# Turning 64 of 96 octets in the second half of batch 0, more zero products in the front, and two tiles' values in a row

## The chip, the cores and the metric

The kernel runs on one core of a Trainium2 chip. The metric is the time of one execution in microseconds; the number that counts is the median over several runs. The span is the time from the first to the last instruction on the core, which the profile sees; the time of a run also has what lies around it.

## The reference

There are four batches, eight heads, 768 positions and 64 numbers per head. Attention goes by chunks of 32 positions: each chunk sees 8 memory keys, its own 32 positions, 16 before and 8 after. A feed-forward part follows.

```python
for c in range(24):
    k_full = concat(mem_k, k[16 before .. 8 after the chunk]); v_full likewise
    a = softmax(q[chunk] @ k_full.T / 8)
    x[chunk] = a @ v_full                     # 8 heads side by side: 512 wide
xn = (x - mean) / sqrt(var + 1e-6) * g_ln
out = x + relu(xn @ w_ch1) @ w_ch2            # 512 -> 2048 -> 512
```

## The kernel before, in words

The 4 x 768 positions make 24 tiles of 128. Three tiles are a unit, so there are eight units, two to a batch. All matmul inputs are 16-bit; sums stand in PSUM in 32 bits.

**Attention of a tile.** `scores` (L278) forms, for two groups of 64 positions, keys times queries into an `att` buffer of PSUM; ScalarE takes the exponentials into `AT` (L294). `values` (L302) multiplies them with `V` into another `att` buffer; a column of ones in `V` gives the sums. `norm` (L314) divides on VectorE (L317, L318), takes the mean (L324) and writes `xn` (L327). `root` (L331) gets the variance: the squares on ScalarE (L333), the inverse root on GpSimd (L336, L340). `turn_x` (L342) turns `xn` into `xT`, in units 0 and 1 with four transposing matmuls (L350) and a copy on ScalarE (L355), later with a DMA. The two `att` buffers are handed out in turn by `slot`, so a product into one waits for whatever still reads it.

**Turning k and q.** `scores` needs k and q with the head's numbers along the partitions. For batches 0 and 1 they are loaded with an octet of positions to a partition (96 octets). `turn_kq` (L183) turns them with a 64-column weight per head and position-in-octet, against the identity, two heads at once in the two column halves of the array: 16 transposing matmuls for a pair of heads. `keep_k` (L195, VectorE) and `keep_q` (L208, ScalarE) then copy out of PSUM into `KT` and `QT`. The first half of batch 0 (octets 0 to 63 for k, 0 to 47 for q) is done in the front. `kq_block` (L215) does the rest of batch 0 in two blocks (128 matmuls) after step 15 of unit 0: it turns all 96 octets, and copies groups 6 to 11 (k from 7).

**The feed-forward of a unit.** Sixteen steps of `up` (L368): four matmuls each and a ReLU, on VectorE and ScalarE in turn (L383, L381). Then twelve steps of `down` (L387), four matmuls each. In unit 0 the order of `down` is by parts: steps 16 to 18 do part 0 of the three tiles and read the first quarter of `w2c`, steps 19 to 21 the second, 22 to 24 the third, 25 to 27 the fourth. The last part adds `xs` on VectorE (L399) and sends the tile out.

**The order of work** is written out by hand. A dictionary `plan` holds, per step of a unit, what is issued after that step's `up` or `down`. `attend` places scores, values, norm and turn_x of the following unit's tiles from four step numbers per tile, and root three steps after turn_x. Each engine runs its instructions in the order of issue.

**The front** (L455 to L562) does the first half of batch 0 and the attention of tiles 0 to 2. `stay_busy` (L360) issues products of zeros (`busy`, 128 x 512) whose result nothing reads. The front's norms, turns and first `up` steps follow one another from tile to tile.

**Loads** are issued on GpSimd's queue in a fixed order (L462 to L505): k and q of the first half, V groups 0 to 5, the four pieces of `w1c`, the second half of k and q, `w2c` 0 and 1, V groups 6 to 9, `w2c` 2, V groups 10 and 11, `w2c` 3. At most eight are under way: the next issue waits until an earlier one has landed.

Of the kernel before, what the change touches and what calls it, by code (L numbers as in the profile page):

```python
# [15 lines left out]
def kernel(  # L16
# [12 lines left out]
    nc = tc.nc  # L29
# [13 lines left out]
    identity = sb.tile([128, 128], FP16, name="identity")  # L43
# [17 lines left out]
    k16 = [t[0:96, 0:4096].rearrange("p (h r d) -> p h r d", h=H, r=8) for t in kraw]  # L61
    q16 = [t[0:96, 0:4096].rearrange("p (h r d) -> p h r d", h=H, r=8) for t in qraw]
# [17 lines left out]
    att = [ps.tile([128, 2, 512], FP32, name=f"att{i}") for i in range(2)]  # L80
# [11 lines left out]
    def free(ap, off, pattern, parts=None):  # L92

        p = list(ap.ap[0]) if parts is None else [ap.ap[0][0], parts]
        return bass.AP(tensor=ap.tensor, offset=ap.offset + off, ap=[p] + [list(x) for x in pattern])

    def as16(t):
        return t.bitcast(FP16)
# [76 lines left out]
    def mem_cols(b):  # L175
        src = memKT[:, 4 * b : 4 * b + 4, :]
        nc.vector.tensor_copy(
            out=free(KT[b % 2], 96, [[KW, 4], [4 * KW, NG], [1, 8]]),
            in_=bass.AP(tensor=src.tensor, offset=src.offset,
                        ap=[list(src.ap[0]), [8, 4], [0, NG], [1, 8]]),  # L180
        )

    def turn_kq(pv, src, j, n):  # L183

        for r in range(8):
            for par in range(2):
                nc.tensor.matmul(  # L187
                    out=pv[64 * par : 64 * par + 64, n * r : n * r + n],
                    lhsT=src[0:n, 2 * j + par, r, :],
                    rhs=identity[0:n, 0:n],  # L190
                    is_transpose=True, start=True, stop=True,
                    tile_position=(0, 64 * par),
                )

    def keep_k(pv, b, j, n, g0, g1, copy=nc.vector.tensor_copy):  # L195

        for ga, gb in ((0, 1), (1, NG - 1), (NG - 1, NG)):
            ga, gb = max(ga, g0), min(gb, g1)
            if ga < gb:
                lo = 0 if ga == 0 else 8 * ga - 2  # L200
                m = 10 if gb == NG else 8 * ga + 9 - lo
                copy(
                    out=free(KT[b % 2], (4 * ga + j) * KW + 16 + 8 * (lo - 8 * ga),
                             [[4 * KW, gb - ga], [8, m], [1, 8]]),
                    in_=free(pv, lo, [[8, gb - ga], [1, m], [n, 8]]),
                )

    def keep_q(copy, pv, b, j, n, g0, g1):  # L208

        copy(  # L210
            out=free(QT[b % 2], (4 * g0 + j) * 64, [[256, g1 - g0], [8, 8], [1, 8]]),
            in_=free(pv, 8 * g0, [[8, g1 - g0], [1, 8], [n, 8]]),
        )

    def kq_block(b, j, g0, g1, kind):  # L215

        pk, pq = slot("att"), None
        if kind == "att":
            pq = slot("att")
            pq = [pq[:, i, :] for i in range(2)]  # L220
        else:
            pq = [slot("mm")[:, :] for i in range(2)]
        for i in range(2):
            turn_kq(as16(pk[:, i, :]), k16[b % 2], j + i, 96)
        for i in range(2):
            turn_kq(as16(pq[i]), q16[b % 2], j + i, 96)

        def keep(i):
            keep_k(as16(pk[:, i, :]), b, j + i, 96, g0 + 1 if g0 else 0, g1)
            keep_q(nc.scalar.copy, as16(pq[i]), b, j + i, 96, g0, g1)  # L230

        keep(0)
        kept_later.append(lambda: keep(1))
# [126 lines left out]
    def stay_busy(n, p=None):  # L360

        p = slot("mm") if p is None else p
        for _ in range(n):
            nc.tensor.matmul(out=p, lhsT=busy[:, 0:128], rhs=busy, start=True, stop=True)  # L364
# [107 lines left out]
    clear_v(0, nc.vector, lambda: clear_k(0), 33)  # L472
    mem_keys()
    mem_cols(0)
    for g in range(3):
        load_v_group(0, g)

# [21 lines left out]
    for g in range(10, NG):  # L499
# [3 lines left out]
        out=memv16[:, 1:B, :, 0:64],  # L503
# [15 lines left out]
        keep_k(first_k[j], 0, j, CUT[0], 0, 7)  # L519
        keep_q(act, first_q[j], 0, j, CUT[1], 0, 6)  # L520
    keep_mem(0, 0, 6, vec)
    stay_busy(3, spare)
    for j in range(2, 4):
        turn_kq(first_k[j], k16[0], j, CUT[0])
    stay_busy(4, spare)
# [8 lines left out]
    vec(out=g_row, in_=banks[2])  # L534
    scores(0, 0)
    scores(0, 1)
    stay_busy(2)
    values(0, 0)
    norm(0, 0)
    stay_busy(3)  # L540
# [24 lines left out]
    for u, tiles in enumerate(units):  # L565
        n = len(tiles)
        following = units[u + 1] if u + 1 < len(units) else []
        plan = {}

        def at(step, fn, *args):  # L570
            plan.setdefault(step, []).append((fn, args))

        def attend(steps, kind="dma"):

            for i, (s0, s1, s2, s3) in enumerate(steps):
                t = following[i]
                at(s0, scores, t // 6, t % 6)
                at(s1, values, t // 6, t % 6)
                at(s2, norm, t % 6, t % 9)
                at(s3, turn_x, u + 1, i, t % 6, kind)  # L580
                at(min(s3 + 3, 27), root, t % 6, t % 9)

        def cross(steps, b, t0, t1, t2):

            for half in range(2):
                at(steps[half], cross_k, b, half, t0, t1)
                at(steps[2 + half], cross_q, b, half, t2 - 3, t2)

        if u == 0:
            at(9, clear_k, 1)  # L590
            at(11, keep_mem, 0, 6, NG, vec)
            at(13, nc.vector.memset, V[0].bitcast(FP32)[:, :, :, 33 : HD // 2], TWO_ONES)
            at(14, nc.vector.memset, memv16[:, :, :, 64:HD], 1.0)
            at(23, clear_v, 1, nc.gpsimd)
            for j in (0, 2):
                at(15, kq_block, 0, j, 6, NG, "mm")
                at(15, keep_rest)
            for t in range(3):
                at(19 + t, root, t, t)
            for h in (0, 4):  # L600
                for which in range(2):
                    at(15, load_kq, 1, which, 0, 96, h, h + 4)
            for g in range(6):
                at(23, load_v_group, 1, g)
            attend(((17, 19, 19, 22), (17, 21, 21, 24), (20, 23, 23, 26)), "att")
            at(26, mem_cols, 1)
            at(26, v_mem, 1)
        elif u == 1:
            for j in (0, 2):
                at(5 + 3 * j, kq_block, 1, j, 0, NG, "att")  # L610
                at(7 + 3 * j, keep_rest)
            for g in range(6, NG):
                at(0, load_v_group, 1, g)
            for t in range(6):
                for which in range(2):
                    at(14, load_tokens, 2, which, t)
            attend(((16, 19, 19, 22), (16, 19, 20, 23), (21, 23, 23, 26)), "att")
        elif following:
            if u in (2, 4):
                attend(((2, 7, 7, 7), (2, 7, 8, 8), (9, 13, 13, 13)))  # L620
            else:
                attend(((9, 14, 14, 14), (9, 14, 15, 15), (16, 20, 20, 20)))
            if u == 2:
                cross((0, 0, 1, 1), 2, 0, 4, 3)
                at(8, mem_cols, 2)
                at(8, k_around, 2, 0, 4)
                for h in range(H):
                    at(8, load_v_head, 2, h)
                cross((14, 14, 15, 15), 2, 4, 6, 6)
            elif u == 3:  # L630
                at(1, v_mem, 2)
                at(1, v_around, 2)
                at(4, k_around, 2, 4, 6)
                for t in range(6):
                    for which in range(2):
                        at(24, load_tokens, 3, which, t)
            elif u == 4:
                for h in range(H):
                    at(0, load_v_head, 3, h)
                cross((14, 14, 15, 15), 3, 0, 4, 3)  # L640
                at(17, mem_cols, 3)
                at(17, v_mem, 3)
                at(17, v_around, 3)
                at(22, k_around, 3, 0, 4)
                cross((20, 21, 24, 25), 3, 4, 6, 6)
            elif u == 5:
                at(2, k_around, 3, 4, 6)
        for step in range(16 + 4 * n):
            if step < 16:
                if u or step > 7:  # L650
                    up(u, n, step)
            else:
                i, part = divmod(step - 16, 4)
                if u == 0:
                    i, part = (step - 16) % 3, (step - 16) // 3
                if following or i < n - 1:
                    down(tiles[i], i, part)
                elif part == 0:
                    down_last(tiles[i], i)
            for fn, args in plan.get(step, ()):  # L660
                fn(*args)
# [30 lines left out]
```

The softmax here doesn't subtract the row's maximum and nothing guards it: scores larger than these inputs give would overflow.

## Time and profile before

| what | us |
|---|---|
| median of 5 runs | 216.72 |
| lowest, highest | 214.76, 219.79 |
| the profiled execution | 216.99 |
| its span, first to last instruction | 215.3 |
| TensorE matmuls busy | 208.9 |
| VectorE, ScalarE, GpSimd busy | 113.5, 91.2, 91.9 |

The mean granted TensorE clock over the span is 0.992 of full speed. Software DMAs (GpSimd's queue) moved 14.38 MB, the others 12.54 MB.

Reading it: lines of the timeline give the start in us, the time from the first start to the last end, engine, line of the kernel, operation, output and inputs with their shapes, and how many instructions the row holds; brackets give the idle time of that engine before it, and what ended it. Matmuls are pipelined, so that the cost of a row is best read from the start of one row to the start of the next. "PE" is TensorE's products, "PEld" its weight loads, "DVE" VectorE, "ACT" ScalarE, "POOL" GpSimd. An answer on DMAs gives their number, size and the time from issue to landing.

### The profile page before, as it was taken

The page shows a single profiled execution, that of the slowest core. Times are in us where ns is not written, and L with a number is a line of the kernel's source. Part 1 is how long each engine was busy: PE and PEld are TensorE (multiplying, and loading weights), DVE is VectorE, ACT ScalarE, POOL GpSimd, SP SyncE. Part 2 cuts the span into 40 slices and gives each one's busy share as a digit, 9 for nine tenths or more (in the row PEclk, how much of TensorE's full clock was granted, in tenths as well). Part 3 has the DMA queues.
Part 4 walks back from the last instruction along what each step waited for, and adds up shares of the span by engine and source line. Part 5 has one row for each costly group of instructions (what it writes and reads, how often), then busy time and mean ns, then how long its engine had stood idle before and what let it go on. Part 6 is the DMA issues. An engine that isn't in the chain of part 4 may idle for free.

```text
span 215.3 us, 5336 instructions
## 1 busy us (share of the span) xinstructions
PE 208.9 (97%) x2173; PEld 124.1 (58%) x2173; DVE 113.5 (53%) x268; ACT 91.2 (42%) x187; POOL 91.9 (43%) x169
## 2 busy tenths in 40 slices
PE   7889999999999999999999999999999999999993
PEld 2545876457755566546654566446644665456553
DVE  4657484585757548524385349324474437534222
ACT  4254535954573676301653067203661265303200
POOL 7992236489999228810004999520042000400000
PEclk9988999999999999999999999999999999999999
DMA  5999999999999959995405999997496201230012
GB/s 77 164 123 201 204 215 182 195 206 229 151 137 171 144 144 128 119 186 156 65 15 87 136 175 155 138 161 113 115 137 184 77 3 24 80 119 0 0 52 97
DMA packets 87611, 27.26 MB, mean 127 GB/s; under 512 B 78289, under 2 KB 84081, under 8 KB 87538
## 3 DMA queue, kind: packets, MB, share of 16 engines
q0 software_dynamic: 62128, 14.38, 74.7%
q1 hardware_dynamic: 25458, 12.54, 27.2%
q8 instruction: 17, 0.28, 0.6%
q14 instruction: 8, 0.07, 0.1%
HBM read 28.84 MB, written 6.29 MB: 163 GB/s over the span
## 4 chain that ended last, share of the span: by engine, by line
PE 91%; DVE 2%; DMA 2%; POOL 1%; issue 1%; ACT 1%; POOLq 0%; DVEq 0%; ACTq 0%
PE mm L375 38%; PE mm L392 38%; PE att L307 4%; PE att L287 3%; DMA kraw<-in_k_dram 2%; PE att L187 2%; PE mm L364 2%; PE mm L410 2%; PE mm L187 1%; DVE xn L327 1%; DVE xs L318 1%; PE att L350 1%; ACT AT L294 1%; PE mm L533 0%; PE att L364 0%
## 5 line engine op out<-in xcount | busy, mean ns | idle before, releaser
L375 PE MATMUL mm<-xT,w1c 128*128 128x384 f16 (+2 forms) x528 | 87.9, 322 | 0.1
L392 PE MATMUL mm<-w2c,rT 128*128 128x512 f16 x368 | 84.2, 379 | 0.0
L375 PEld LDWEIGHTS <-w1c 128*128 128x128 f16 x528 | 57.9, 114 | 24.8 <-issue 0.6
L381 ACT ACTIVATE rT<-mm 128x384 f16<-128x384 f32 (+2 forms) x66 | 31.7, 484 | 75.3 <-PE mm L375 53.9
L392 PEld LDWEIGHTS <-rT 128*128 128x128 f16 x368 | 34.5, 98 | 38.4
L383 DVE TENSOR_SCALAR rT<-mm 128x384 f16<-128x384 f32 (+2 forms) x66 | 35.6, 542 | 33.7 <-PE mm L375 33.4
L399 DVE SCALAR_TENSOR_TENSOR osb<-mm,rstd,xs 128x512 f32<-128x512 f32 x23 | 17.3, 751 | 42.2 <-PE mm L392 30.9
L294 ACT ACTIVATE AT<-att,band 104x512 f16<-104x512 f32 x48 | 29.5, 688 | 11.9 <-PE att L287 10.2
L336 POOL TENSOR_SCALAR veps<-squares 128x1 f32<-128x1 f32 x24 | 5.1, 213 | 50.0 <-ACT junk L333 48.7
L116 POOL DMA_DIRECT2D V<-in_v_dram x24 | 18.5, 776 | 11.6 <-DMA w1c<-in_moe_w_ch_dram 8.5
L333 ACT ACTIVATE junk<-xs,nmean 128x512 f16<-128x512 f32 x24 | 17.4, 724 | 7.7 <-DVE nmean L324 6.9
L327 DVE SCALAR_TENSOR_TENSOR xn<-xs,nmean,g_row 128x512 f16<-128x512 f32 x24 | 18.0, 752 | 0.9
L318 DVE SCALAR_TENSOR_TENSOR xs<-att,rec 128x512 f32<-128x512 f32 x24 | 16.6, 691 | 0.8
L274 POOL COPY KT<-KT 128x128 f16<-128x128 f16 (+4 forms) x16 | 4.4, 305 | 26.0 <-DMA KT<-kraw 26.0
L340 POOL TENSOR_TENSOR rstd<-veps,mhalf 128x1 f32<-128x1 f32 x24 | 13.7, 572 | 2.0
L122 POOL DMA_DIRECT2D V<-in_v_dram x16 | 12.0, 778 | 0.4 <-issue 0.4
L307 PEld LDWEIGHTS <-AT 104*64 104x64 f16 x384 | 7.7, 112 | 7.6 <-issue 3.5
L247 POOL DMA_DIRECT2D qraw<-in_q_dram x12 | 11.2, 936 | 0.0
L247 POOL DMA_DIRECT2D kraw<-in_k_dram x12 | 11.2, 934 | 0.0
L364 PE MATMUL mm<-busy 128*128 128x512 f16 x26 | 9.2, 488 | 1.2 <-DVE counts L456 1.2
L317 DVE RECIPROCAL rec<-att 128x8 f32<-128x8 f32 x24 | 4.9, 203 | 10.4 <-ACT AT L294 5.7
L307 PE MATMUL att<-V,AT 104*64 104x65 f16 x384 | 9.7, 199 | 0.7 <-ACT AT L294 0.7
(76 smaller groups left out, 117.4 us busy)
## 6 DMA issues: line engine op xcount, KB each, us to landing
out_dram<-osb SPq DMA_DIRECT2D x23, 256.0 KB, 2.8
V<-in_v_dram POOLq DMA_DIRECT2D x36, 96.0 KB, 6.2
w1c<-in_moe_w_ch_dram POOLq DMA_DIRECT2D x4, 512.0 KB, 10.1
w2c<-in_moe_w_ch_dram POOLq DMA_DIRECT2D x4, 512.0 KB, 14.4
kraw<-in_k_dram POOLq DMA_DIRECT2D x12, 128.0 KB, 5.3
qraw<-in_q_dram POOLq DMA_DIRECT2D x12, 128.0 KB, 5.8
qraw<-in_q_dram POOLq DMA_DIRECT2D x3, 384.0 KB, 12.5
kraw<-in_k_dram POOLq DMA_DIRECT2D x3, 256.0 KB, 5.1
```

Source lines behind the costliest of these rows:

```text
L116: nc.gpsimd.dma_start(out=V[b % 2][r : r + hi - lo, g, :, 0:64], in_=dram(v, b * H * HS + lo * D, [[64, hi - lo], [HS, H], [1, 64]]),)
L247: nc.gpsimd.dma_start(out=free(dst, 512 * t, [[64, H], [1, 64]]), in_=dram(src, b * H * HS + 128 * t * D, [[D, 128], [HS, H], [1, 64]]),)
L294: nc.scalar.activation(out=free(a, 32 * c, [[512, 2], [64, 8], [1, 32]], KR), in_=free(p, 32 * c, [[512, 2], [64, 8], [1, 32]], KR), func= ...
L307: nc.tensor.matmul(out=p[64 * gg : 64 * gg + 64, h // 4, c0 : c0 + 65], lhsT=AT[t % 3][0:KR, h % 2, 4 * gg + h // 2, :], rhs=V[b % 2][0:KR ...
L318: nc.vector.scalar_tensor_tensor(out=x.rearrange("p (h d) -> p h d", h=H), in0=free(p, 0, [[128, H], [1, 64]]), scalar=1.0, in1=free(r, 0, ...
L327: nc.vector.scalar_tensor_tensor(out=xn[i], in0=x, scalar=nmean[i], in1=g_row, op0=ALU.add, op1=ALU.mult,)
L333: nc.scalar.activation(out=junk, in_=xs[xi], func=ACTF.Square, bias=nmean[i], accum_out=squares[i],)
L375: nc.tensor.matmul(out=p, lhsT=free(w, i, [[4, 128]]), rhs=xT[u % 2][:, dt, lo:hi], start=(dt == 0), stop=(dt == 3),)
L381: nc.scalar.activation(out=o, in_=p, func=ACTF.Relu)
L383: nc.vector.tensor_scalar(out=o, in0=p, scalar1=0.0, scalar2=None, op0=ALU.max)
L392: nc.tensor.matmul(out=p, lhsT=rT[hc][:, 128 * i : 128 * i + 128], rhs=w2c[hc // 4][:, hc % 4, :], start=(hc == 0), stop=(hc == 15),)
L399: nc.vector.scalar_tensor_tensor(out=o, in0=p, scalar=rstd[t % 9], in1=xs[t % 9], op0=ALU.mult, op1=ALU.add,)
```

## The change

Three things change.

1. The second half of batch 0 is turned for octets 32 to 95 alone. A new function takes `identity[0:96, 32:96]` as the moving operand of a plain product instead of the whole identity in a transposing one. The result is 64 columns wide and 32-bit in PSUM, where it was 96 columns and 16-bit. `keep_k` and `keep_q` read with the new spacing and base. The number of matmuls (128) and of copies stays. Batch 1, which is turned whole, is as before.
2. Seven more zero products: two after the memory keys (L167), two more (five for three) before the second k turn, three more (five for two) after the scores of tiles 0 and 1.
3. Unit 0's plan for tiles 3, 4, 5. Scores: after steps 17, 17, 21 (before 17, 17, 20). Values: 20, 20, 23 (before 19, 21, 23). Norm: 20, 21, 24 (before 19, 21, 23). Turn: 23, 24, 26 (before 22, 24, 26). Root of tile 3: after 26 (before 25). On VectorE and on GpSimd the order of instructions stays; on ScalarE the squares of tile 2 come ahead of the exponentials of tile 5 and the squares of tile 1 stay ahead of them; on TensorE the values of tiles 3 and 4 are issued without a step between them. The values of tile 4 now have the other `att` buffer, so that the scores of tile 5 take the one that tile 3's values had.

```diff
+    def pick_kq(pv, src, j, lo, hi):
+        n = hi - lo
+        for r in range(8):
+            for par in range(2):
+                nc.tensor.matmul(
+                    out=pv[64 * par : 64 * par + 64, n * r : n * r + n],
+                    lhsT=src[0:hi, 2 * j + par, r, :],
+                    rhs=identity[0:hi, lo:hi],
+                    start=True, stop=True, tile_position=(0, 64 * par),
+                )
...
     def kq_block(b, j, g0, g1, kind):
...
-        for i in range(2):
-            turn_kq(as16(pk[:, i, :]), k16[b % 2], j + i, 96)
-        for i in range(2):
-            turn_kq(as16(pq[i]), q16[b % 2], j + i, 96)
+        pk = [pk[:, i, :] for i in range(2)]
+        if g0:
+            n, base = 64, 32
+            for p, src in ((pk, k16[b % 2]), (pq, q16[b % 2])):
+                for i in range(2):
+                    pick_kq(p[i], src, j + i, base, base + n)
+        else:
+            n, base = 96, 0
+            pk, pq = [as16(p) for p in pk], [as16(p) for p in pq]
+            for p, src in ((pk, k16[b % 2]), (pq, q16[b % 2])):
+                for i in range(2):
+                    turn_kq(p[i], src, j + i, n)
...
     mem_cols(0)
+    stay_busy(2)
...
-    stay_busy(3, spare)
+    stay_busy(5, spare)
     for j in range(2, 4):
         turn_kq(first_k[j], k16[0], j, CUT[0])
...
     scores(0, 1)
-    stay_busy(2)
+    stay_busy(5)
     values(0, 0)
...
-            attend(((17, 19, 19, 22), (17, 21, 21, 24), (20, 23, 23, 26)), "att")
+            attend(((17, 20, 20, 23), (17, 20, 21, 24), (21, 23, 24, 26)), "att")
```

More of the change, by code (lines that the diff above doesn't have):

```diff
@@ L193, in turn_kq, with keep_k @@
                 )
-    def keep_k(pv, b, j, n, g0, g1, copy=nc.vector.tensor_copy):
+    def pick_kq(pv, src, j, lo, hi):
[8 more added lines that the diff above has]
+                )
+    def keep_k(pv, b, j, n, g0, g1, copy=nc.vector.tensor_copy, base=0):
         for ga, gb in ((0, 1), (1, NG - 1), (NG - 1, NG)):
@@ L204, in keep_k, with keep_q @@
                              [[4 * KW, gb - ga], [8, m], [1, 8]]),
-                    in_=free(pv, lo, [[8, gb - ga], [1, m], [n, 8]]),
+                    in_=free(pv, lo - base, [[8, gb - ga], [1, m], [n, 8]]),
                 )
-    def keep_q(copy, pv, b, j, n, g0, g1):
+    def keep_q(copy, pv, b, j, n, g0, g1, base=0):
         copy(
             out=free(QT[b % 2], (4 * g0 + j) * 64, [[256, g1 - g0], [8, 8], [1, 8]]),
-            in_=free(pv, 8 * g0, [[8, g1 - g0], [1, 8], [n, 8]]),
+            in_=free(pv, 8 * g0 - base, [[8, g1 - g0], [1, 8], [n, 8]]),
         )
@@ L222, in kq_block @@
             pq = [slot("mm")[:, :] for i in range(2)]
-        for i in range(2):
-            turn_kq(as16(pk[:, i, :]), k16[b % 2], j + i, 96)
-        for i in range(2):
-            turn_kq(as16(pq[i]), q16[b % 2], j + i, 96)
+        pk = [pk[:, i, :] for i in range(2)]
[10 more added lines that the diff above has]
+                    turn_kq(p[i], src, j + i, n)
         def keep(i):
-            keep_k(as16(pk[:, i, :]), b, j + i, 96, g0 + 1 if g0 else 0, g1)
-            keep_q(nc.scalar.copy, as16(pq[i]), b, j + i, 96, g0, g1)
+            keep_k(pk[i], b, j + i, n, g0 + 1 if g0 else 0, g1, base=base)
+            keep_q(nc.scalar.copy, pq[i], b, j + i, n, g0, g1, base=base)
         keep(0)
```

## The prediction

> **What bounds the kernel now.** I read the page first, then TensorE's order of work in the front and in unit 0, then the granted clock in stretches, and last the DMA landings that the same stretches wait for. The page:
>
> ```profile
> PE 208.9 (97%) x2173; PEld 124.1 (58%) x2173; DVE 113.5 (53%) x268; ACT 91.2 (42%) x187; POOL 91.9 (43%) x169
> ...
> PE 91%; DVE 2%; DMA 2%; POOL 1%; issue 1%; ACT 1%; POOLq 0%; DVEq 0%; ACTq 0%
> ```
>
> TensorE is busy for 97% of the span and is 91% of the chain that ended last. A microsecond taken from it should come off the end, unless something stands close behind it. All edits lie before 48 us, so the first question is what TensorE waits for there. The timeline of TensorE in the front:
>
> ```profile
> 4.83 0.25 PE L167 MATMUL mm<-identity,memk 128*64 128x64 f16 x4
> 5.60 0.69 PE L187 MATMUL mm<-identity,kraw 64*64 64x64 f16 x32 [0.51 <-DMA kraw<-in_k_dram]
> ...
> 7.51 0.82 PE L364 MATMUL att<-busy 128*128 128x512 f16 x3
> 8.80 0.69 PE L187 MATMUL mm<-identity,kraw 64*64 64x64 f16 x32 [0.47 <-DMA kraw<-in_k_dram]
> ...
> 12.63 0.60 PE L364 MATMUL mm<-busy 128*128 128x512 f16 x2
> 13.89 0.44 PE L307 MATMUL att<-V,AT 104*64 104x65 f16 x16 [0.65 <-ACT AT L294]
> 14.27 1.46 PE L364 MATMUL mm<-busy 128*128 128x512 f16 x3
> ...
> 21.55 0.39 PE L350 MATMUL mm<-identity,xn 128*128 128x128 f16 x4
> ```
>
> There are three idle gaps, 0.51, 0.47 and 0.65 us. They are where the change puts zero products. The three zero products at 14.27 need 1.39 us until the next row (15.66), where the three at 18.06 need 0.74. The granted clock, in stretches (the last three numbers are PEclk, DMA share and GB/s):
>
> ```profile
> 31.27:34.69 3.42, 3.42 (x132) 2.99 (x131) 3.00 (x9) 1.96 (x5) 0.72 (x1) 1.00 1.64 170
> 10.80:14.21 3.41, 2.76 (x70) 1.42 (x64) 1.25 (x2) 2.12 (x4) 3.41 (x5) 1.00 1.55 102
> ...
> 14.21:17.62 3.41, 3.41 (x46) 1.55 (x41) 2.90 (x10) 1.51 (x4) 2.57 (x5) 0.50 1.16 174
> ```
>
> TensorE ran at half clock for 3.41 us from 14.21, just after the stretch that holds the 0.65 us gap. Unit 0's stretch:
>
> ```profile
> 31.45 0.87 PE L187 MATMUL att<-identity,kraw 96*64 96x96 f16 x32
> ...
> 34.29 1.90 PE L392 MATMUL mm<-w2c,rT 128*128 128x512 f16 x8
> ...
> 41.18 0.44 PE L307 MATMUL att<-V,AT 104*64 104x65 f16 x16
> 41.56 1.04 PE L392 MATMUL mm<-w2c,rT 128*128 128x512 f16 x4
> ...
> 45.08 1.89 PE L392 MATMUL mm<-w2c,rT 128*128 128x512 f16 x8
> ```
>
> No gap shows from 31 to 48 us. But the projection's parts 2 and 3 (steps 22 and 25, at 41.56 and 45.08) each read a piece of w2c for the first time. The DMA answers for the issues of those pieces, and POOL's timeline:
>
> ```profile
> w2c<-in_moe_w_ch_dram POOLq DMA_DIRECT2D x1, 512.0 KB, 12.4
> ```
>
> ```profile
> w2c<-in_moe_w_ch_dram POOLq DMA_DIRECT2D x1, 512.0 KB, 9.6
> ```
>
> ```profile
> 28.43 0.56 POOL L157 DMA_DIRECT2D w2c<-in_moe_w_ch_dram  x1
> ...
> 34.91 0.56 POOL L157 DMA_DIRECT2D w2c<-in_moe_w_ch_dram  x1 [1.47 <-DMA w2c<-in_moe_w_ch_dram]
> ...
> 41.09 0.67 POOL L106 DMA_DIRECT2D qraw<-in_q_dram  x1 [2.87 <-DMA w2c<-in_moe_w_ch_dram]
> ```
>
> The third piece, issued at 28.43, lands 12.4 us later, at 40.8. The fourth, issued at 34.91, lands 9.6 us later, at 44.5 (44.46 at full resolution). TensorE reaches them at 41.56 and 45.08: only 0.7 and 0.6 us late. POOL's issues wait for earlier DMAs, never for TensorE, and the page's DMA row stands at 9 from slice 2 through slice 10. So this stream does not move when TensorE gets faster. It is the floor behind the bound.
>
> **The change, part by part.**
>
> *Seven zero products.* A run of n of them takes 0.11 + 0.216 n until the next small product (four from 9.43 to 10.39 are 0.96). Two after the row at 4.83 end near 5.50, before 5.60. Five from 7.51 end near 8.70, before 8.80. Five from 12.63 end near 13.82, before 13.89. Cost nothing, under the cover of two landings of kraw and of the exp; if all three covers were gone, 7 x 0.216 = 1.5 us.
>
> What they can buy is the half clock at 14.21. The Trainium skill, in "TensorE: Matmul & The Clock Gate" ("Why this matters for your kernels"), says the clock falls back after an idle gap of more than some 3 us. By that rule gaps of 0.5 us are harmless and the seven products buy 0. The row says otherwise: the largest gap was 0.65 and the clock fell. In 10.80 to 14.21, besides 0.65 us idle, 1.05 us went to the product of L533, which uses one row of the array. The two stretches of the same length before it, with 0.58 and 0.47 idle but no such product, did not fall. Three more full-array products in that stretch should keep the clock; I take the row.
>
> At full clock, by rows: norm of tile 1 on VectorE is bound by VectorE itself (tile 0 from 14.45 to 16.36, tile 1 to 18.34), but tile 2's began at 19.29, waiting for its values. Counting from 14.27 with full-clock lengths, the values of tile 2 come at 17.46, so that norm starts at 18.38 and the turn of tile 2 at 20.36 instead of 21.55: 1.19 us. If the clock falls anyway, 0.
>
> *Second half turned for 64 octets.* 128 products took 34.29 - 31.45 = 2.84 us; a block of 32 is 0.68, 21 ns each. Nearest rows for 64 columns: the values (65 columns, 104 rows, the same two column halves) cost 0.25 us for sixteen more (0.63 for 32 at 65.73, 0.38 for 16), 15.7 ns each; scores, 14.6; the turns of 64 columns in the front, some 16.5. So 128 x 15.5 + 0.1 = 2.1, between 2.0 and 2.2: a gain of 0.65 to 0.85, I take 0.75. The copies now read 32-bit PSUM. VectorE's 512 elements took 692 ns from 32-bit PSUM and 528 took 696 from 16-bit, ScalarE's 384 took 484 and 482, so nothing is added. They end about 0.3 us before the scores that wait for them; a tenth more on eight copies would still be hidden.
>
> The same page (Part 4) says that transposes do not count as busy for the clock. By that, turning into plain products would also guard the clock after this stage, worth half of 3.41 us. But 31.27 to 34.69 is 83% transposes and the clock stayed 1.00 afterwards. I add nothing.
>
> *Values of tiles 3 and 4 in a row.* Two single groups cost 2 x 0.375, a double 0.63; and one switch from a projection group to small products goes (0.97 against 0.86). Gain 0.23. Scores of tile 5 now follow one step after them and need the att buffer that tile 3's norm reads; by the rows (VectorE starts 0.55 after the values' start, frees it 0.95 later) it is free at 1.50, and the scores come at 1.59. The turn of tile 3 needs tile 4's norm to have read: free at 3.60, wanted at 3.67. Cost 0, at most 0.2 if these margins go. The squares of tile 2 now stand ahead of tile 5's exp on ScalarE: 0.9 us, and the exp still ends 0.3 before its values. No DMA is moved on any queue.
>
> *Sum for TensorE:* 1.19 + 0.75 + 0.23 = 2.17 us earlier at step 25. On the way the fourth piece of w1c (landed 27.35, then wanted at 27.56) and the first of w2c (32.15, wanted at 32.35) are met with 0.2 us to spare.
>
> *What is late next.* Step 22 would come at about 39.4 and waits for the third piece of w2c until 40.84 (landing plus 0.04, as at 8.76 to 8.80): a new stall of 1.4 us. Steps 22 to 24 with their turns and values take 3.52 us, so step 25 comes at 44.36 and waits for the fourth piece until 44.50. Before: 45.08. **Left of 2.17 us: 0.58.** It stays 0.58 if the half clock comes anyway, or if the products cost 16.5 ns, because 0.98 is still above the floor. After 48 us nothing else gives: batch 1's first k and q landed 3.5 us before they were turned, and TensorE's starts are dense to the end.
>
> The profiled execution is 216.99 us (span 215.3): 216.4 after. The median of the five shown is 0.27 lower, so **216.1 us**.
>
> **Rivals.**
> - *The stream lands earlier in other executions* and TensorE's gain shows in full: 2.17 us, 214.5. For it: one of the five took 214.76, which the floor of this trace does not allow. Against it: the stream is saturated.
> - *No change.* If most executions keep the clock, they sit on the floor already, at 44.50. Then nothing is left to gain: 216.7. For it: the five runs spread by 5 us, so the profiled one need not be typical. Against: it is near their median, and it was half-clocked.
> - *Slower: the new stall trips the clock.* 1.4 us idle at 39.4 lies in one stretch of 3.41 (38.10 to 41.51, counting on from 14.21). Then 41.51 to 44.93 runs at half clock: of the 3.52 us to step 25, 0.67 is done before, 1.71 within, 1.14 after, so step 25 comes at 46.07, 1.0 us later than before: 217.7. It decides if the trip point lies above the 58% dense work left in that stretch. For it: 10.80 to 14.21 fell with 0.65 idle. Against: that stretch had only 1.7 us of ordinary products, 50%.
>
> **How the numbers follow.** Chances: floor 0.60, full gain 0.14, no change 0.13, clock tripped 0.13. The likeliest alone spans 215.4 to 216.8. The executions before spread over 5 us, so each case is blurred by some 0.5. For 8 in 10, with both outer cases at their middle: 214.6 to 217.7. A measurement of this kernel tells about 1%, 2.2 us, from no change. Faster by more than that needs the full gain and a little luck: 0.10. Slower, 219 or more, needs the clock tripped and another loss: 0.04. Within: 0.86.
>
> **What would show it.** Right: PEclk 1.00 through 14 to 18 us; the turn of tile 2 near 20.4; the 128 products near 2.1 us; values in one row of 32; a wait of L392 on the DMA of w2c of over 1 us; step 25 within 0.1 us of the fourth landing. Wrong: no wait on w2c (landings moved), a 0.50 stretch after that wait, or scores of tile 5 waiting for VectorE.

## The result and the profile after

| | before | changed |
|---|---|---|
| median of the runs, us | 216.95 (77 runs) | 216.34 (40 runs) |
| lowest, highest | 214.76, 219.79 | 215.13, 217.58 |
| profiled execution, us | 216.99 | 216.54 |
| its span | 215.3 | 214.8 |

The ratio is 0.9981, with a 95% interval from 0.9967 to 0.9996: 0.4 us faster, well inside 1%. The prediction's likeliest case was 0.58 us. All ratios here leave out executions more than 1.5% above the fastest of their kernel, which drops 11 of the 77 of the kernel before and none of the changed kernel's, so that they show less of the gain than the medians of all runs do, 0.61 us.

The page of the changed kernel, TensorE's row and the chain that ended last, by engine and by line:

```profile
PE 209.4 (97%) x2180; PEld 123.8 (58%) x2180; DVE 113.0 (53%) x268; ACT 91.4 (43%) x187; POOL 91.3 (43%) x169
...
PE 75%; DMA 13%; POOL 7%; DVE 2%; issue 1%; POOLq 0%; DVEq 0%
PE mm L412 34%; PE mm L395 33%; DMA w2c<-in_moe_w_ch_dram 13%; PE att L327 3%; POOL V L116 2%; PE att L307 2%; PE mm L430 2%; POOL w1c L151 1%; PE att L187 1%; POOL kraw L106 1%; POOL qraw L106 1%; DVE xn L347 1%; DVE xs L338 1%; DVE rT L403 0%; PE att L370 0%
```

TensorE is busy for 97% as before, but the chain no longer follows it through the start: 13% of the span is now the load of w2c, and 7% GpSimd, which issues the loads. The bound of the first 45 us has changed hands. TensorE's timeline shows where (brackets: idle time before the row and what ended it):

```profile
1.25 4.45 PE L384 MATMUL mm<-busy 128*128 128x512 f16 x10 [1.25 <-DVE counts L476]
5.63 0.32 PE L167 MATMUL mm<-identity,memk 128*64 128x64 f16 x4
5.88 0.79 PE L384 MATMUL mm<-busy 128*128 128x512 f16 x2
6.60 0.69 PE L187 MATMUL mm<-identity,kraw 64*64 64x64 f16 x32
...
8.38 1.25 PE L384 MATMUL att<-busy 128*128 128x512 f16 x5
9.56 0.69 PE L187 MATMUL mm<-identity,kraw 64*64 64x64 f16 x32
...
14.65 0.44 PE L327 MATMUL att<-V,AT 104*64 104x65 f16 x16
...
20.94 0.39 PE L370 MATMUL mm<-identity,xn 128*128 128x128 f16 x4
...
30.84 0.69 PE L200 MATMUL att<-identity,kraw 96*64 96x64 f16 x32
...
32.99 1.90 PE L412 MATMUL mm<-w2c,rT 128*128 128x512 f16 x8
...
38.09 0.84 PE L327 MATMUL att<-V,AT 104*64 104x65 f16 x32
38.86 1.04 PE L412 MATMUL mm<-w2c,rT 128*128 128x512 f16 x4
...
40.53 1.89 PE L412 MATMUL mm<-w2c,rT 128*128 128x512 f16 x8 [0.29 <-DMA w2c<-in_moe_w_ch_dram]
...
43.82 0.39 PE L370 MATMUL att<-identity,xn 128*128 128x128 f16 x4
44.64 1.89 PE L412 MATMUL mm<-w2c,rT 128*128 128x512 f16 x8 [0.43 <-DMA w2c<-in_moe_w_ch_dram]
```

The waits on w2c are in the brackets at 40.53 and 44.64 (steps 22 and 25). The DMA answers for the issues of these two pieces, at 28.93 and 35.16, end in the time to landing:

```profile
w2c<-in_moe_w_ch_dram POOLq DMA_DIRECT2D x1, 512.0 KB, 11.6
```

```profile
w2c<-in_moe_w_ch_dram POOLq DMA_DIRECT2D x1, 512.0 KB, 9.4
```

They land at 40.5 and 44.6 us, and TensorE goes on 0.04 us later. From step 25 to the end of the span it takes 170.2 us in both kernels. So all that the end gained between these two executions is the move of step 25, from 45.08 to 44.64. The fourteen traces of this document agree: from step 25 on each takes 169.9 to 170.2 us, plus what it waits for one later copy (`V<-V`, below). The clock after the 14th microsecond (PEclk is the third number from the end):

```profile
14.21:17.62 3.41, 3.41 (x62) 1.74 (x60) 2.28 (x7) 2.52 (x5) 2.68 (x5) 1.00 1.13 171
```

### The profile page after: what moved, and what is told of

Read it like the earlier page. It is cut to its first block, busy times and chain, and to the rows that moved or that the text cites. A ratio compares the mean times of both kernels' runs of the same rounds, so it can differ in the third digit from the quotient of the medians.

```text
span 214.8 us, 5353 instructions
## 1 busy us (share of the span) xinstructions
PE 209.4 (97%) x2180; PEld 123.8 (58%) x2180; DVE 113.0 (53%) x268; ACT 91.4 (43%) x187; POOL 91.3 (43%) x169
## 4 chain that ended last, share of the span: by engine, by line
PE 75%; DMA 13%; POOL 7%; DVE 2%; issue 1%; POOLq 0%; DVEq 0%
PE mm L412 34%; PE mm L395 33%; DMA w2c<-in_moe_w_ch_dram 13%; PE att L327 3%; POOL V L116 2%; PE att L307 2%; PE mm L430 2%; POOL w1c L151 1%; PE att L187 1%; POOL kraw L106 1%; POOL qraw L106 1%; DVE xn L347 1%; DVE xs L338 1%; DVE rT L403 0%; PE att L370 0%
## 5 line engine op out<-in xcount | busy, mean ns | idle before, releaser
L116 POOL DMA_DIRECT2D V<-in_v_dram x24 | 19.2, 806 | 11.0 <-DMA w1c<-in_moe_w_ch_dram 7.7
L122 POOL DMA_DIRECT2D V<-in_v_dram x16 | 12.0, 768 | 0.2
L384 PE MATMUL mm<-busy 128*128 128x512 f16 x31 | 10.4, 468 | 1.2 <-DVE counts L476 1.2
L307 PEld LDWEIGHTS <-KT 64*128 64x128 f16 x384 | 6.5, 95 | 5.9 <-issue 5.8
## 6 DMA issues: line engine op xcount, KB each, us to landing
w2c<-in_moe_w_ch_dram POOLq DMA_DIRECT2D x4, 512.0 KB, 14.1
qraw<-in_q_dram POOLq DMA_DIRECT2D x3, 384.0 KB, 13.4
```

Source lines behind the costliest of these rows:

```text
L116: nc.gpsimd.dma_start(out=V[b % 2][r : r + hi - lo, g, :, 0:64], in_=dram(v, b * H * HS + lo * D, [[64, hi - lo], [HS, H], [1, 64]]),)
```

## The experiments

**1. Is the landing of w2c a floor?** Two kernels load only its first two pieces and use them twice (their output is another), so that no new piece is waited for in steps 22 and 25. Two others delay the fourth piece by one more load.

```diff
+    w2c[2:4] = w2c[0:2]            # after_two, before_two
-    load_w2(2)
-    load_w2(3)
```

```diff
+    nc.gpsimd.dma_start(out=more, in_=...)     # after_late, before_late: 512 KB
     load_w2(3)
```

before_two:

> The kernel before, with only two pieces of w2c loaded: the third and fourth are not, and parts 2 and 3 of the projection use the first two again, so that the result is another. Floor theory (the landings of w2c stand 0.6 us ahead of TensorE before the change, 0.0 ahead of it after): TensorE was the later one, so nothing changes; part 3 of unit 0 starts at 45.1 us as before, time 0.0 +- 0.3 us. Rival (DMA traffic as such slows the kernel): a megabyte less makes it faster by 1 us or more.

after_two:

> The changed kernel, with only two pieces of w2c loaded; the third and fourth are not, and parts 2 and 3 of the projection use the first two again, so that the result is another. Floor theory: no wait on w2c is left, step 22 follows at about 40.2 and part 3 starts at 43.5 to 43.9 instead of 44.64, so 0.8 to 1.1 us faster than the changed kernel and 1.2 to 1.5 us faster than before (ratio 0.993 to 0.9945). Rival (TensorE's gain of the change is only the 0.4 to 0.6 us that showed, and the waits on w2c are idle time that costs nothing): same time as the changed kernel, 0.4 us under before.

after_late:

> The changed kernel with one more load of 512 KB, into a tile that nothing reads, issued just ahead of the fourth piece of w2c. Floor theory: the fourth piece lands some 2.5 us later (one piece follows the other by 2.5 us), TensorE waits for all of it: 2.5 us slower than the changed kernel, 2.0 us slower than before (ratio 1.009). Rival (the transfer is hidden, TensorE alone sets the end): as the changed kernel, 0.4 us under before.

before_late:

> The kernel before with one more load of 512 KB, into a tile that nothing reads, issued just ahead of the fourth piece of w2c. Floor theory: the piece lands 2.5 us later, of which 0.6 us is hidden behind TensorE: 1.9 us slower than before (ratio 1.009), so no slower than the changed kernel with the same load. The gap of 0.4 us between the two kernels closes to 0.0 +- 0.3. Rival (TensorE alone sets the end): no change, and the gap between the two kernels stays.

| kernel | ratio to before | interval | step 25 starts, us | fourth piece lands |
|---|---|---|---|---|
| before_two | 1.0000 | 0.9979 to 1.0021 | 45.36 | none |
| after_two | 0.9943 | 0.9922 to 0.9965 | 43.62 | none |
| after_late | 1.0087 | 1.0056 to 1.0118 | 45.76 | 45.72 |
| before_late | 1.0098 | 1.0066 to 1.0129 | 46.58 | 46.54 |

In its direction each of the four is the floor's answer, and after_two is 0.8 us under the changed kernel's ratio. The two late kernels have six runs each. TensorE's timeline at step 25, first of after_two, then of after_late (with a later row), then of before_late:

```profile
43.39 0.39 PE L371 MATMUL att<-identity,xn 128*128 128x128 f16 x4
43.62 1.89 PE L413 MATMUL mm<-w2c,rT 128*128 128x512 f16 x8
```

```profile
43.62 0.39 PE L371 MATMUL att<-identity,xn 128*128 128x128 f16 x4
45.76 1.67 PE L413 MATMUL mm<-w2c,rT 128*128 128x512 f16 x7 [1.75 <-DMA w2c<-in_moe_w_ch_dram]
...
110.27 0.70 PE L328 MATMUL att<-V,AT 104*64 104x65 f16 x32 [0.79 <-DMA V<-V]
```

```profile
44.34 0.39 PE L351 MATMUL att<-identity,xn 128*128 128x128 f16 x4
46.58 0.81 PE L393 MATMUL mm<-w2c,rT 128*128 128x512 f16 x3 [1.85 <-DMA w2c<-in_moe_w_ch_dram]
```

Without the landings the changed kernel shows what its TensorE saves: 0.57% of 216.8, 1.2 us. With the later load both kernels are slower by about 2 us, and the changed one has no lead that can be told. Not all of that passed through the fourth piece: in after_late's trace it landed 1.1 us later than in the changed kernel's, not 2.5 as expected, and about as much went to waits for V<-V (0.79 and 0.27 us).

The megabyte that before_two leaves out is worth nothing, because TensorE was the later one there: it came to step 25 at 45.36. The experiment excludes the rival of a TensorE-bound start for the changed kernel, and the one of traffic as such. But half clock is not what made TensorE late in that trace (its mean clock is 1.000). These rows did:

```profile
19.87 1.06 PE L376 MATMUL mm<-xT,w1c 128*128 128x256 f16 x8 [1.05 <-DMA w1c<-in_moe_w_ch_dram]
...
28.48 2.79 PE L376 MATMUL mm<-xT,w1c 128*128 128x384 f16 x16 [0.35 <-DMA w1c<-in_moe_w_ch_dram]
...
34.31 0.33 PE L188 MATMUL mm<-identity,qraw 96*64 96x96 f16 x7 [0.32 <-issue]
```

So the same stream is a floor earlier too, at the first and fourth pieces of w1c, when TensorE comes early. before_late, at full clock as well, waited 0.70 us for the first piece.

**2. The three parts alone, and two without the third.**

```diff
+    stay_busy(2)                   # zero_only: after mem_cols(0);
+    stay_busy(5, spare)            #   and 5 for 3, 5 for 2 as in the change
```

```diff
+                    pick_kq(p[i], src, j + i, base, base + n)   # pick_only
```

```diff
+            attend(((17, 20, 20, 23), (17, 20, 21, 24), (21, 23, 24, 26)), "att")   # plan_only
```

zero_only:

> The kernel before with the seven zero products alone. Theory: they keep the clock (no half-clock stretch after 14 us), the turn of tile 2 comes 0.6 to 1.2 us earlier than at 21.55; part 3 of unit 0 meets the fourth piece of w2c at 44.5 +- 0.2: 0.4 to 0.6 us faster than before. Rival (they only fill gaps; the clock falls all the same): PEclk shows 0.50 after 14 us again and the time is 0 to 0.5 us slower.

pick_only:

> The kernel before with the turn for 64 octets alone. Theory: the 128 products take 2.15 us instead of 2.84, part 3 starts at the landing of the fourth piece of w2c or 0.7 us earlier than before, whichever is later: 0.4 to 0.7 us faster where the clock falls in the front, 0 to 0.3 where it does not. Rival (the copies from 32-bit PSUM or the drain of the plain products eat it): 0 to 0.5 us slower, with a wait of the scores on VectorE's copies.

plan_only:

> The kernel before with the new plan of unit 0 alone. Theory: values of tiles 3 and 4 in one row of 32 for 0.63 us, part 3 starts 0.2 us earlier: 0.1 to 0.25 us faster, not to be told from no change by the time. Rival (a wait of the scores of tile 5 or of the turn of tile 3 takes its place): 0.1 to 0.5 us slower, with that wait in the trace.

pick_plan (the changed kernel less the zero products):

> The changed kernel without the seven zero products (turn for 64 octets and new plan alone). In earlier runs the kernel before lost the clock in about a third of its executions (mean clock under 0.996) and then took about 1 us more span than where it kept it; with the seven zero products hardly any did. Theory (the products' worth is to save those executions; what the turn and the plan save, 0.9 us of TensorE, goes into the waits on w2c where the clock is kept): executions that keep the clock have a span of 214.6 to 214.9 like the changed kernel, those that lose it are at most 0.4 us later, since the 0.9 us are there to cover it; median 0 to 0.2 us from the changed kernel. Rival (the products made the whole gain): as the kernel before, 0.4 us over the changed one, and its lost executions at 215.9.

| kernel | ratio to before | interval | executions under 0.996 of the clock |
|---|---|---|---|
| zero_only | 0.9993 | 0.9973 to 1.0014 | 0 of 22 |
| pick_only | 0.9986 | 0.9956 to 1.0016 | 3 of 14 |
| plan_only | 1.0013 | 0.9980 to 1.0046 | 8 of 14 |
| pick_plan | 0.9999 | 0.9972 to 1.0026 | 11 of 22 |

No part can be told from no change by its time. The clock column can be told. Counting all executions, kernels with the seven products fell under 0.996 once in 171 executions; the kernel before, in the sessions of the experiments, 55 times in 169, and the other kernels without the products 32 times in 78. Of the 169, 114 kept the clock with a median span of 215.0 us; 35 were near 0.992 (one half-clock stretch of 3.41 us), with 215.5; 20 at 0.984 or just under it (two), with 217.0. The changed kernel's median is 214.7. The rival for zero_only (the clock falls all the same) is out. In its trace step 25 comes 0.04 us after the fourth landing (44.34):

```profile
44.38 1.89 PE L392 MATMUL mm<-w2c,rT 128*128 128x512 f16 x8
```

plan_only's trace has the double stretch. Its clock before, in and after it:

```profile
8.28:11.69 3.41, 3.10 (x70) 1.76 (x70) 2.08 (x4) 1.27 (x4) 3.33 (x6) 1.00 1.77 124
11.69:18.51 6.82, 6.79 (x91) 3.37 (x91) 4.18 (x11) 3.68 (x6) 5.18 (x8) 0.50 1.32 154
18.51:22.00 3.49, 3.46 (x40) 2.14 (x38) 2.04 (x7) 1.17 (x2) 0.80 (x1) 1.00 1.22 199
```

Its turn of tile 2 came at 22.14, and step 25 at 45.45, 1.4 us after the fourth piece (44.02). Its values in a row took the expected time:

```profile
39.98 0.70 PE L307 MATMUL att<-V,AT 104*64 104x65 f16 x32
40.61 1.04 PE L392 MATMUL mm<-w2c,rT 128*128 128x512 f16 x4
```

0.63 us, and no wait of tile 5's scores behind them. pick_plan missed its expectation: its eleven executions with a lost clock had a median span of 216.6, against 214.9 for those that kept it, not at most 0.4 us more, and its ratio is that of the kernel before, as its rival said. Its trace has two half-clock stretches too, and TensorE came to step 25 1.1 us after the fourth piece (44.55):

```profile
13.59:20.42 6.83, 6.58 (x75) 3.30 (x77) 3.63 (x10) 3.20 (x6) 3.99 (x7) 0.50 1.16 176
```

```profile
45.66 1.89 PE L412 MATMUL mm<-w2c,rT 128*128 128x512 f16 x8
```

pick_only's trace, at full clock, met the fourth piece late (43.98, landing 43.37) and still ended only 0.2 us ahead of before's. It lost its lead in two places:

```profile
32.97 0.29 PE L200 MATMUL mm<-identity,qraw 96*64 96x64 f16 x7 [1.09 <-issue]
...
43.98 1.89 PE L412 MATMUL mm<-w2c,rT 128*128 128x512 f16 x8
...
104.36 3.44 PE L395 MATMUL mm<-xT,w1c 128*128 128x384 f16 x20
108.73 0.70 PE L327 MATMUL att<-V,AT 104*64 104x65 f16 x32 [0.93 <-DMA V<-V]
```

For the first the profile names no releaser ("issue"). before_two (0.32) and before_late (0.21) stop at the same seven products, the other traces do not; the cause stays open. Without it TensorE would have been ahead of the landing.

The second is batch 2's copy of V's neighbours, 330 KB in rows of 14 KB on SyncE's queue. In before its second part was issued at 101.42 and landed at 108.28, 0.55 us ahead of its use. So there is a second transfer half a microsecond behind TensorE. Four of the fourteen traces wait for it, in batch 2 or 3 (pick_only, pick_plan, after_late, fill_around).

**3. Can the waits be used?** fill puts 8 products of unit 1 into the wait of step 25; fill_two is the same with both groups ahead of both ReLUs; around_early issues V<-V earlier; fill_around has both.

```diff
+            at(24, up_ahead, 1, (0, 1))          # ups of tile 3 alone: 2 x 4 products, 128 columns
-                    up(u, n, step)
+                    up(u, n, step, 1 if u == 1 and step < 2 else 0)
...
-                at(1, v_around, 2)               # around_early: from unit 3, with v_mem,
+                at(24, v_around, 2)              #   to unit 2
```

fill:

> The changed kernel with useful work put into the wait for the fourth piece of w2c: the first two ups of unit 1 for tile 3 alone (8 products of 128 columns, 0.45 us) are issued after step 24, and left out of steps 0 and 1 of unit 1, which then have 256 columns instead of 384. Floor theory: part 3 still starts at the landing, the wait shrinks by 0.45 us, unit 1's first two steps take 0.43 us less: 0.3 to 0.45 us faster than the changed kernel, 0.8 us under before. Rival (the wait is not the bound): as the changed kernel or 0.1 slower.

fill_two:

> As the kernel fill, whose second group of products waited 0.85 us for the ReLU of the first in the same PSUM bank; here both groups are issued ahead of both ReLUs. Theory: the group takes 0.45 us in place of 1.24 and fits into the wait for the fourth piece of w2c, part 3 starts at the landing, unit 1's first steps take 0.43 us less, of which 0.15 may go to a wait for the third tile's PSUM bank: 0.3 us faster than the changed kernel, ratio to before 0.9965 +- 0.002. Rival (the wait on w2c sets nothing): ratio 0.998 to 1.000.

around_early:

> The changed kernel with the copies V<-V of batch 2 issued after step 24 of unit 2 instead of step 1 of unit 3, ahead of the third out of unit 2. In two of the traces the values at 109 us waited 0.8 to 0.9 us for that copy; in the others it landed about 0.5 us ahead of them. Theory (a second floor, reached in some executions): issued 2 to 3 us earlier, it is never waited for; 0.1 to 0.3 us faster than the changed kernel in the median, with a smaller spread. Rival (those waits were chance, or the copy now takes longer beside the outs): no change.

fill_around:

> Both of the last two edits on the changed kernel. Theory: the gains add, 0.4 to 0.6 us faster than the changed kernel, ratio to before 0.995 to 0.9965. Rival (a next wait takes them): ratio 0.9975 or more.

| kernel | ratio to before | interval | median, us | median span |
|---|---|---|---|---|
| fill | 1.0002 | 0.9981 to 1.0023 | 216.92 | 215.2 |
| fill_two | 0.9962 | 0.9939 to 0.9985 | 215.96 | 214.25 |
| around_early | 0.9955 | 0.9930 to 0.9979 | 216.37 | 214.7 |
| fill_around | 0.9939 | 0.9915 to 0.9962 | 215.78 | 214.05 |

fill failed. TensorE's timeline of fill, then of fill_two:

```profile
44.56 0.39 PE L409 MATMUL mm<-xT,w1c 128*128 128x128 f16 x4
45.58 0.39 PE L409 MATMUL mm<-xT,w1c 128*128 128x128 f16 x4 [0.63 <-ACT rT L414]
45.80 1.89 PE L425 MATMUL mm<-w2c,rT 128*128 128x512 f16 x8
```

```profile
44.20 0.61 PE L409 MATMUL mm<-xT,w1c 128*128 128x128 f16 x8
44.70 1.89 PE L426 MATMUL mm<-w2c,rT 128*128 128x512 f16 x8
```

In fill the second group waited for ScalarE's ReLU of the first, since both lie in one PSUM tile; step 25 came 1.1 us after the landing (44.66). In fill_two the same eight products take 0.5 us, and step 25 starts 0.04 us after its landing (44.66). In this execution the filling is free, as the floor theory says. By its time fill_two is faster than before, but its interval overlaps the changed kernel's, so that a gain over that one is not shown. around_early's median equals the changed kernel's (216.37 and 216.34), so its gain is not shown; its ratio is lower because the kernel before had a median of 217.23 beside it. fill_around has the lowest median of the kernels that do all of the work, 0.6 us under the changed one's; its interval lies wholly under before and ends just short of that of the changed kernel (0.9962 against 0.9967), which was measured in another session. Beside fill_two it is not told apart. Its own trace had no wait to fill at step 25 (the fourth piece had landed at 43.33), and it shows where the next microsecond hides:

```profile
44.00 1.89 PE L426 MATMUL mm<-w2c,rT 128*128 128x512 f16 x8
...
150.50 3.44 PE L395 MATMUL mm<-xT,w1c 128*128 128x384 f16 x20
155.01 0.70 PE L327 MATMUL att<-V,AT 104*64 104x65 f16 x32 [1.07 <-DMA V<-V]
```

The last row waits for the same copy for batch 3, which the edit left in its place. Batch 2's, which it moved, was not waited for.

## Why the prediction was right, and where not

**The floor: right.** Step 25 starts 0.04 us after the fourth landing, as forecast, and the waits stand where the prediction put them. For the changed kernel experiment 1 settles it from both sides. The sizes of the waits were off: 0.29 us at step 22 where 1.4 was forecast, 0.43 at step 25 where it was 0.14. The floor stands earlier as well: the prediction counted on 0.2 us to spare at the fourth piece of w1c and the first of w2c, and fill waited 0.58 us for the one, fill_two 0.35 for the other.

**The seven products "cost nothing": wrong.** The cover was read from one execution, in which the zero products began to take 0.22 us each instead of 0.43 at about 4 us. In the changed kernel's trace the first ten all took 0.43 us (the PEclk column reads 1.00 there, it does not show the first microseconds): 4.38 us to the next row instead of 3.59. The two new ones behind them took 0.72 instead of 0.54, and the first k turn started at 6.60, 1.1 us after its data (5.50). The five products then held the second turn until 9.56; its data were there at 8.12. In the eight traces with the products the first k turn lies at 6.1 to 6.8 us, in the six without at 5.6 to 5.9. At the values of tile 0 this was 0.76 us (14.65 for 13.89); over the traces they lie at 14.1 to 14.9 us with the products and at 13.4 to 14.0 without.

**They keep the clock: right, and the row beat the rule.** The 3.41 us before the fall held no more than 0.65 us idle in before, 0.31 in plan_only and 0.40 in pick_plan, where the Trainium skill ("TensorE: Matmul & The Clock Gate", "Why this matters for your kernels") asks for a gap of more than some 3 us. Nor is it the gap alone. pick_only had the same 0.65 us gap at the same place (first row) and kept the clock, and before_late kept it after the stretch of the second row, with 0.70 us idle:

```profile
13.57 0.44 PE L327 MATMUL att<-V,AT 104*64 104x65 f16 x16 [0.65 <-ACT AT L314]
...
16.45:19.86 3.41, 2.71 (x31) 1.16 (x29) 3.12 (x9) 1.49 (x3) 0.29 (x1) 1.00 1.20 195
```

In all three falls the stretch also held most or all of the one-row product that the prediction pointed to; zero_only's trace, with that product and hardly any idle time, kept the clock. So the seven products are shown to keep it; which of them, and what tips it, is not.

From the values of tile 0 to the turn of tile 2 it took 6.30 us instead of 7.66: 1.36, forecast 1.19. Less the 0.76 before it, 0.61 of the 1.19 remained (the turn at 20.94, forecast near 20.4).

**The turn for 64 octets: right.** 30.84 to 32.99 is 2.15 us, forecast 2.1 (0.70 gained, forecast 0.75). The copies from 32-bit PSUM cost nothing more (VectorE's eight took 2.41 us, before 2.61).

**The values in a row: the size right, a wait missed.** The row took 0.77 us instead of 0.63, because tile 4's second V group, issued at 26.94, landed at 38.48, behind the row's start at 38.09. The DMA answer for it:

```profile
V<-in_v_dram POOLq DMA_DIRECT2D x1, 96.0 KB, 11.5
```

The prediction had checked that buffer's norms and exponentials, and not the landings of V. It is one more place where the same stream was close.

**The sum.** 0.61 + 0.70 + 0.23 - 0.14 = 1.4 us of TensorE, not 2.17. The end does not show the difference, because both are more than the floor leaves: 0.44 us at step 25, forecast 0.58, as the fourth piece landed 0.13 later (44.59 for 44.46). That the forecast came so near the measured 0.4 us is in part luck. The floor hid the error in the sum, and the forecast was read from an execution with one half-clock stretch, which is neither the usual one nor the worst.

**"It stays 0.58 if the half clock comes anyway": wrong.** It assumed one half-clock stretch. There can be two in a row, 6.8 us, and then TensorE is late by more than the other two edits save: pick_plan has both of these edits, and in its trace step 25 is still 1.1 us behind the landing. Its ratio of 0.9999 shows no gain.

**"After 48 us nothing else gives": wrong in some executions.** The copy V<-V, 0.55 us ahead of its use in before, was waited for in four of the fourteen traces, for 0.74 to 1.07 us in all.

**The rival "no change" had half of the truth.** Two thirds of before's executions keep the clock, and they stand at 215.0, 0.3 us over the changed kernel, which ran in another session; zero_only, beside which they stood at 214.85, is at 214.8. What the change removes besides is the third that did not. How the measured 0.4 us divides between the two cannot be settled: the intervals of the parts are 0.4 us or more wide to each side. The rival "slower" did not come: after_late waited 1.75 us before step 25 and its clock stayed at 1.00.

## What to carry to other kernels

Before adding up what a busy engine saves, list for each of its next first uses of loaded data how long ago that data had landed: the smallest of these margins caps the gain, here 0.6 us of a forecast 2.2, if the load is not issued earlier when the engine gets faster. Work that fills a wait is free only as long as the wait is there in every execution, so read its length in more than one trace, and once with a late clock. A wait that has become the bound can take work that comes later anyway, if that work brings no wait of its own.

## What was not expected of the hardware

The clock of TensorE fell with gaps of no more than 0.65 us, in about a third of the executions of one and the same program, in the traces for 3.41 or 6.83 us; it did not fall after one gap of 1.75 us between dense products (after_late). In the three traces the fall (14.21, 11.69 and 13.59 us) comes three, two and two times 3.41 us after the moment when the first products began to run at full speed (about 4.0, 4.9 and 6.8). That moment varies from one execution to the next. It may be why one program keeps the clock in one execution and loses it in another, by what happens to fall into one such stretch; no run here tests that. The second part of the copy V<-V took 6.9 us from issue to landing in one execution (before) and 8.3 in another (pick_only).
